# A fused linear-attention and MoE kernel on one core: another fixed order of its steps, and most weights' signs made by ScalarE

## The chip, the cores and the metric

The kernel runs on one core of a Trainium2 chip. Its time is the device time of one launch, in microseconds (us). Three runs of the kernel before took 515.26, 516.27 and 516.82 us; their median is 516.27 us.

## The reference, cut to what matters

For each of 4 x 8 heads a 48 x 48 state runs over 768 tokens; its output, put side by side over the heads, goes through one feed-forward layer.

```python
for t in range(S):                       # S = 768, per head, D = 48
    state = alpha[t][:, None] * state + outer(k[t], v[t])
    y[t] = q[t] @ state
x = y as (3072 tokens, 384)
h = x @ w_in                             # (384, 2048)
sp = maximum(h, 0) + log1p(exp(-abs(h)))
g = h * erf(sp)
out = g @ w_out                          # (2048, 384)
```

`w_in` and `w_out` are float64 and come to the chip as pairs of 32-bit words.

## The kernel before, in words

The program is one flat list of steps, written out in the string `ORDER`. A step is a method and its indices, and most are one instruction, or one block of matmuls. The loop at the end walks the list. `Queue` ties each instruction of TensorE (PE), VectorE (DVE), ScalarE (ACT) and SyncE (SP, which issues the loads and stores) to the one before it on its engine, so the list fixes the order on each engine. Between engines only data and buffers decide.

**Attention.** There are 24 chunks (64 tokens of two batches each); the step's index is the chunk. `la lk lq lv` load alpha, k, q, v. On DVE `sb` and `sa` are the scans of alpha, `kk` and `qq` scale k and q, `mk` masks the scores, `td` and `ta` decay the state and add to it. On PE `pn` transposes k, `ps` makes the scores (32 matmuls), `qt` and `sv` the two parts of the output (64 each), `pu` the state's update (32). `xh` (ACT) rounds the output to x_hi. The rest x_lo is either one subtraction on DVE (`xl`), or two matmuls with minus identity that take x_hi off in PSUM (`xp`, PE) and a copy (`xe`, ACT).

**Feed-forward.** Two chunks make a block of 256 tokens; there are 12 blocks, the first index of the MoE's steps; the second is one of 4 groups of 512 hidden columns, the third a half of a group. `hm` is 18 matmuls (three products of hi and lo parts), evicted from one of two PSUM buffers by `he` (ACT) or `hd` (DVE). Then, per group, ACT runs `u` (tanh), `n1 n2 n3` (ln, ln, exp) and `g` (gelu), and DVE `ma mb z1 z2`, all on 128 x 1024. `ga` (ACT) or `gd` (DVE) rounds a half, `gl` (DVE) makes the rest of it, and `om` is 12 matmuls into the output's accumulators: 4 with gh and wo_hi, 4 with gh and wo_lo, 4 with gl and wo_hi. `oe` (ACT) or `ob` (DVE) evicts an accumulator, `od` stores it. `u` and `g` need one table set of ACT, `n1 n2 n3` another; `need` puts a table load wherever the list goes over from one to the other.

**Weights.** `wl` loads a piece, 12 of `w_in` (i, 512 columns) and 16 of `w_out` (o, 384 columns). From the 64-bit words a piece is put together: `wy` (ACT) takes exponent and mantissa from the high word, `wc` (ACT) or `wv` (DVE) the three bits from the low word, `wa` (DVE) joins them by a shift and an or, `wb` (DVE) ors the sign in. Then `wh` (ACT) or `wk` (DVE) rounds to hi, and lo comes from `wq` (DVE), or from `wp` (three matmuls in an `hm` buffer, PE) and a copy `we` (ACT). Methods `wd` and `wf` are in the class, but no step of the list before calls them: `wd` (ACT) writes the high word, scaled, as float16 into the upper 16 bits of each word, which sets the sign there, and `wf` (ACT) writes the three bits as int16 into the lower 16 bits. With both, `wb` is not needed.

`dw_n` runs n matmuls that compute nothing used. `f1 f2 f3` make the flag that the end of the program branches on.

Of the kernel before, what the change touches and what calls it, by code (L numbers as in the profile page):

```python
# [41 lines left out]
wqo_0 he_0_2_0 whi_10 wyo_1 wao_1 sb_4 wqi_9 n1_0_0 xh_2 xl_2 pn_2 kn_2 n2_0_0 wqi_10 ic_3 hm_0_1_1 he_0_1_1
n3_0_0 hm_0_2_1 he_0_2_1 wbo_1 rc_4 who_1 pu_2 ps_3 wlo_3 wyo_3 lq_4 lk_4 wlo_7 mk_3 ta_2 qt_3 ma_0_0 g_0_0 sa_4
wlo_6 mb_0_0 wqo_1 hm_0_3_0 z1_0_0 wco_3 wao_3 lv_3 sv_3 xh_3 xl_3 kk_4 pn_3 he_0_3_0 wyo_7 hm_0_3_1 kn_3 ic_4
z2_0_0 td_4 lk_5 he_0_3_1 la_5 wco_7 wco_6 hm_1_0_0 qq_4 wlo_9 wyo_6 sb_5 u_0_1 wao_7 wbo_3 ga_0_0_0 gl_0_0_0
hm_1_1_0 he_1_0_0 ga_0_0_1 gl_0_0_1 wao_6 u_0_2 n1_0_1 pu_3 ps_4 n1_0_2 rc_5 n2_0_1 qt_4 om_0_0_0 hm_1_0_1 wbo_7
who_7 mk_4 ta_3 lv_4 sv_4 sa_5 td_5 who_3 wqo_3 kk_5 n3_0_1 he_1_1_0 ma_0_1 wbo_6 pn_4 wqo_7 mb_0_1 he_1_0_1
n2_0_2 kn_4 lq_5 qq_5 n3_0_2 who_6 ma_0_2 la_6 xh_4 xl_4 om_0_0_1 wyo_9 wco_9 wao_9 wqo_6 mb_0_2 g_0_1 z1_0_1
wlo_11 wyo_11 hm_1_2_0 he_1_2_0 wbo_9 lk_6 z2_0_1 lv_5 hm_1_3_0 he_1_3_0 g_0_2 z1_0_2 pu_4 wco_11 ps_5 mk_5 lq_6
wlo_8 wco_8 wyo_8 wlo_4 z2_0_2 qt_5 wao_8 ga_0_1_1 wlo_5 hm_1_3_1 he_1_3_1 hm_1_2_1 wco_4 wlo_13 wyo_4 wao_11  # L50
u_0_3 gl_0_1_1 hm_1_1_1 wlo_10 u_1_0 wbo_8 ta_4 ga_0_2_0 om_0_1_1 wbo_11 sv_5 ic_5 who_9 wqo_9 who_8 n1_0_3
gl_0_2_0 wqo_8 om_0_2_0 sb_6 he_1_1_1 lv_6 wao_4 td_6 ga_0_1_0 gl_0_1_0 pn_5 wbo_4 xh_5 he_1_2_1 rc_6 xl_5
hm_2_1_0 hm_2_1_1 wyo_5 who_11 wqo_11 wco_5 wko_4 sa_6 wao_5 qq_6 qt_6 kn_5 pu_5 wyo_10 wlo_14 wco_10 wbo_5
wao_10 kk_6 ps_6 n2_0_3 ga_0_2_1 n1_1_0 who_5 wqo_5 he_2_1_0 wqo_4 om_0_1_0 n3_0_3 gl_0_2_1 wbo_10 ma_0_3
he_2_1_1 wvo_13 hm_2_0_0 mb_0_3 n2_1_0 wyo_13 n3_1_0 wao_13 mk_6 ta_5 wbo_13 who_10 wqo_10 g_0_3 z1_0_3 he_2_0_0
hm_2_0_1 who_13 wqo_13 z2_0_3 wco_14 ma_1_0 pn_6 he_2_0_1 wyo_14 wlo_15 wco_15 wyo_15 wao_14 om_0_2_1 kn_6 sv_6
ga_0_3_0 gl_0_3_0 pu_6 wao_15 ga_0_3_1 gl_0_3_1 xh_6 wbo_14 lv_7 om_0_3_0 u_1_1 lk_7 wbo_15 g_1_0 mb_1_0
hm_2_2_0 ic_6 la_7 who_15 wqo_15 who_14 wqo_14 om_0_3_1 u_1_2 n1_1_2 oe_0_1 od_0_1 oe_0_0 hm_2_2_1 z1_1_0 z2_1_0
ga_1_0_0 sb_7 lq_7 rc_7 gl_1_0_0 gd_1_0_1 n1_1_1 lq_8 xl_6 sa_7 gl_1_0_1 om_1_0_0 n2_1_2 n2_1_1 om_1_0_1
he_2_2_0 qq_7 kk_7 hm_2_3_0 n3_1_1 td_7 ma_1_1 mb_1_1 n3_1_2 he_2_2_1 ps_7 mk_7 qt_7 hm_2_3_1 g_1_1 u_1_3 z1_1_1  # L60
z2_1_1 u_2_1 ic_7 ga_1_1_0 sv_7 xh_7 ta_6 la_8 ga_1_1_1 lv_8 ma_1_2 pn_7 gl_1_1_0 om_1_1_0 gl_1_1_1 om_1_1_1
sb_8 he_2_3_0 mb_1_2 g_1_2 n1_1_3 he_2_3_1 n2_1_3 n3_1_3 lk_8 xl_7 hm_3_0_0 hm_3_0_1 z1_1_2 z2_1_2 rc_8 gd_1_2_0
gl_1_2_0 om_1_2_0 ma_1_3 he_3_0_0 ga_1_2_1 gl_1_2_1 om_1_2_1 g_1_3 he_3_0_1 td_8 hm_3_1_0 hm_3_1_1 mb_1_3 sa_8
u_2_0 n1_2_0 lk_9 n2_2_0 z1_1_3 z2_1_3 gd_1_3_1 kk_8 ga_1_3_0 la_9 gl_1_3_0 om_1_3_0 n3_2_0 lq_9 qq_8 kn_7
n1_2_1 n2_2_1 n3_2_1 he_3_1_0 od_0_0 he_3_1_1 gl_1_3_1 pu_7 ps_8 ma_2_0 qt_8 mb_2_0 om_1_3_1 sb_9 ma_2_1 mb_2_1
g_2_1 z1_2_1 ob_1_0 od_1_0 u_2_2 oe_1_1 hm_3_2_0 mk_8 z2_2_1 hm_3_2_1 g_2_0 ic_8 rc_9 gd_2_1_1 u_2_3 n1_2_2 sv_8
gd_2_1_0 gl_2_1_1 gl_2_1_0 xh_8 n2_2_2 ta_7 om_2_1_0 pn_8 z1_2_0 he_3_2_0 ic_9 sa_9 om_2_1_1 he_3_2_1 z2_2_0
gd_2_0_1 gl_2_0_1 n3_2_2 n1_2_3 kk_9 xl_8 lv_9 ma_2_2 hm_3_3_0 hm_3_3_1 ga_2_0_0 n2_2_3 n3_2_3 kn_8 qq_9 g_2_2
om_2_0_1 mb_2_2 td_9 qt_9 pu_8 ps_9 ma_2_3 gl_2_0_0 om_2_0_0 u_3_1 u_3_0 z1_2_2 he_3_3_1 mk_9 sv_9 g_2_3
he_3_3_0 lq_10 n1_3_0 z2_2_2 gd_2_2_0 gl_2_2_0 om_2_2_0 od_1_1 la_10 mb_2_3 gd_2_2_1 xh_9 sb_10 xl_9 hm_4_0_0  # L70
rc_10 n1_3_1 n2_3_1 n2_3_0 gl_2_2_1 n3_3_0 n3_3_1 sa_10 he_4_0_0 ta_8 ma_3_0 hm_4_0_1 he_4_0_1 om_2_2_1 g_3_0
z1_2_3 z2_2_3 ga_2_3_0 mb_3_0 u_3_2 ga_2_3_1 z1_3_0 hm_4_2_0 hm_4_2_1 ma_3_1 lk_10 kk_10 u_3_3 qq_10 he_4_2_0
la_11 gl_2_3_0 g_3_1 n1_3_3 pn_9 kn_9 gl_2_3_1 n2_3_3 n3_3_3 om_2_3_0 td_10 om_2_3_1 oe_2_1 oe_2_0 qt_10 lk_11
z2_3_0 mb_3_1 z1_3_1 hd_4_2_1 z2_3_1 gd_3_1_0 sb_11 gl_3_1_0 ga_3_0_1 pu_9 ps_10 mk_10 ta_9 gl_3_0_1 n1_3_2
n2_3_2 n3_3_2 ic_10 rc_11 ic_11 hm_4_1_0 he_4_1_0 lv_11 hm_4_1_1 td_11 he_4_1_1 om_3_1_0 ma_3_2 pn_10 ga_3_0_0
gl_3_0_0 u_4_0 om_3_0_1 od_2_1 g_3_2 sa_11 u_4_1 mb_3_2 z1_3_2 ga_3_1_1 ma_3_3 g_3_3 lq_12 gl_3_1_1 z2_3_2
hm_4_3_0 hm_4_3_1 om_3_1_1 om_3_0_0 u_4_2 n1_4_2 ga_3_2_1 kd_10 lv_10 pu_10 n1_4_1 n2_4_1 kk_11 la_12 mb_3_3
lq_11 qq_11 ps_11 sv_10 xh_10 sb_12 he_4_3_1 gl_3_2_1 om_3_2_1 gd_3_2_0 gl_3_2_0 mk_11 ta_10 rc_12 xl_10 z1_3_3
z2_3_3 gd_3_3_1 od_2_0 pn_11 n1_4_0 n2_4_0 om_3_2_0 kn_11 gl_3_3_1 n3_4_0 ga_3_3_0 gl_3_3_0 qt_11 ma_4_0 pu_11
sa_12 n3_4_1 lk_12 mb_4_0 sv_11 he_4_3_0 n2_4_2 ma_4_1 xh_11 xl_11 lk_13 mb_4_1 kk_12 om_3_3_1 n3_4_2 g_4_1  # L80
td_12 g_4_0 la_13 z1_4_1 z1_4_0 z2_4_1 om_3_3_0 ob_3_0 od_3_0 u_4_3 qq_12 hm_5_0_0 he_5_0_0 hm_5_0_1 he_5_0_1
u_5_0 n1_5_0 z2_4_0 ga_4_0_0 gd_4_0_1 hm_5_1_0 lv_12 he_5_1_0 ma_4_2 mb_4_2 hm_5_1_1 oe_3_1 he_5_1_1 od_3_1
gl_4_0_0 qt_12 n1_4_3 ps_12 mk_12 hm_5_2_0 om_4_0_0 gl_4_0_1 sb_13 lq_13 hm_5_3_0 n2_4_3 ic_12 ta_11 n3_4_3
ma_4_3 pn_12 lk_14 he_5_2_0 n2_5_0 n3_5_0 mb_4_3 kk_13 ma_5_0 g_4_3 mb_5_0 ga_4_1_1 td_13 gl_4_1_1 u_5_1
om_4_0_1 he_5_3_0 hm_5_2_1 g_4_2 he_5_2_1 rc_13 sa_13 z1_4_2 hm_5_3_1 om_4_1_1 g_5_0 gd_4_1_0 gl_4_1_0 om_4_1_0
la_14 z1_4_3 z2_4_2 gd_4_2_0 kn_12 gl_4_2_0 u_5_2 n1_5_1 lq_14 ic_13 z2_4_3 sv_12 n2_5_1 ga_4_2_1 om_4_2_0 xh_12
xl_12 qq_13 gl_4_2_1 pu_12 ps_13 n1_5_2 n3_5_1 ma_5_1 qt_13 mk_13 g_5_1 mb_5_1 z1_5_1 ga_4_3_1 gl_4_3_1 om_4_2_1
lv_13 sv_13 xh_13 xl_13 he_5_3_1 z2_5_1 ga_4_3_0 gl_4_3_0 sb_14 om_4_3_1 ta_12 td_14 n2_5_2 lv_14 n3_5_2
hm_6_1_0 he_6_1_0 hm_6_2_0 he_6_2_0 rc_14 sa_14 ic_14 qq_14 ma_5_2 pn_13 kn_13 mb_5_2 u_5_3 z1_5_0 z2_5_0
ga_5_1_1 g_5_2 om_4_3_0 oe_4_0 oe_4_1 od_4_1 hm_6_0_0 he_6_0_0 hm_6_0_1 n1_5_3 n2_5_3 lk_15 hm_6_1_1 n3_5_3  # L90
kk_14 z1_5_2 z2_5_2 gl_5_1_1 pu_13 ps_14 la_15 hd_6_0_1 u_6_0 hd_6_1_1 hm_6_2_1 he_6_2_1 mk_14 ta_13 gd_5_2_0
# [855 lines left out]
```

## Time and profile before

| | us |
|---|---|
| median of three runs | 516.27 |
| span of the profiled execution, first to last instruction | 513.9 |
| median less span (what lies around it) | 2.4 |
| PE busy | 504.0 |
| weight loads of PE (PEld) busy | 481.7 |
| DVE busy | 488.2 |
| ACT busy | 465.8 |

The clock granted to TensorE was 1.00 of full speed in the whole span. Three engines are busy for over nine tenths of the time. A busy PE in this profile is one with a matmul under way, so what a step costs is read from the start of one to the start of the next, not from its length. An instruction of DVE or ACT is recorded until its last write, and the next one starts about 0.1 us before that.

### The profile page before, as it was taken

To read this page: it belongs to the slowest core of one execution; us is meant where nothing else is said; L and a number is where in the kernel's file an instruction comes from. 1 tells how busy PE (TensorE), PEld (TensorE's weight loads), DVE (VectorE), ACT (ScalarE), POOL (GpSimd) and SP (SyncE) were. 2 spreads that over 40 slices of the span, in tenths; PEclk is the share of its full clock that TensorE was granted. 3 is DMA by queue.
4 is the path that set the end of the run, shared out by engine and by line. 5 is a ranking of instruction groups with operands and counts; after the bars stand their busy time and mean duration, and the time that the engine had idled before them with its cause. 6 is when DMAs were issued, how large, how long until landed. Compare 5 with 4: busy or idle time off the path is not lost.

```text
span 513.9 us, 16869 instructions
## 1 busy us (share of the span) xinstructions
PE 504.0 (98%) x7465; PEld 481.7 (94%) x7465; DVE 488.2 (95%) x655; ACT 465.8 (91%) x637; POOL 6.5 (1%) x41
## 2 busy tenths in 40 slices
...
GB/s 324 401 200 176 117 188 131 97 81 60 58 74 44 22 99 78 45 73 83 23 78 107 80 41 60 85 15 44 68 111 54 90 58 32 3 1 32 0 32 34
DMA packets 21387, 43.69 MB, mean 85 GB/s; under 512 B 2368, under 2 KB 5440, under 8 KB 21312
## 3 DMA queue, kind: packets, MB, share of 16 engines
...
q8 instruction: 59, 0.97, 0.8%
q14 instruction: 16, 0.13, 0.1%
...
## 4 chain that ended last, share of the span: by engine, by line
PE 64%; DVE 18%; ACT 12%; issue 4%; DMA 1%; POOL 1%; DVEq 0%; POOLq 0%; ACTq 0%
PE acc L211 29%; PE h__112 L211 13%; PE h__111 L211 12%; PE both L211 4%; PE py L211 4%; DVE t L211 2%; DVE gl__104 L211 1%; ACT L211 1%; DVE gl__103 L211 1%; DVE w__98 L211 1%; DVE w__100 L211 1%; PE warm L211 1%; ACT w__97 L211 1%; DMA s__87<-in_moe_w_out_dram 1%; DVE w__97 L211 1%
## 5 line engine op out<-in xcount | busy, mean ns | idle before, releaser
L211 ACT ACT_TABLE_LOAD x64 | 82.1, 1283 | 1.9 <-PEq L901 0.9
L211 PE MATMUL acc<-wo_hi,gh__102 128*128 128x384 f32 x192 | 44.7, 346 | 0.1
L211 PE MATMUL acc<-wo_hi,gh__101 128*128 128x384 f32 x192 | 43.9, 348 | 0.1
L211 PE MATMUL acc<-wo_lo,gh__102 128*128 128x384 f32 x192 | 43.0, 337 | 0.2 <-DVE wo_lo L211 0.2
L211 PE MATMUL acc<-wo_hi,gl__104 128*128 128x384 f32 x192 | 43.1, 337 | 0.0
L211 PE MATMUL acc<-wo_lo,gh__101 128*128 128x384 f32 x192 | 41.6, 336 | 0.0
L211 PE MATMUL acc<-wo_hi,gl__103 128*128 128x384 f32 x192 | 41.6, 337 | 0.0
L211 PEld LDWEIGHTS acc<-wo_lo,gh__102 128*128 128x128 f32 x192 | 34.2, 188 | 0.5 <-DVE wo_lo L211 0.5
L211 PEld LDWEIGHTS acc<-wo_hi,gl__104 128*128 128x128 f32 x192 | 34.3, 188 | 0.0
L211 PEld LDWEIGHTS acc<-wo_hi,gl__103 128*128 128x128 f32 x192 | 34.0, 188 | 0.2 <-DVE gl__103 L211 0.2
L211 PEld LDWEIGHTS acc<-wo_lo,gh__101 128*128 128x128 f32 x192 | 34.1, 188 | 0.0
L211 PEld LDWEIGHTS acc<-wo_hi,gh__101 128*128 128x128 f32 x192 | 31.6, 188 | 1.9 <-DVE gh__101 L211 0.4
L211 PEld LDWEIGHTS acc<-wo_hi,gh__102 128*128 128x128 f32 x192 | 32.6, 188 | 0.8 <-DVE gh__102 L211 0.2
L211 DVE TENSOR_TENSOR_SCAN B<-raw_a,back 128x520 f32<-128x520 f32 x24 | 29.6, 1233 | 4.0 <-POOL T L266 3.9
L211 DVE TENSOR_TENSOR_SCAN A<-raw_a,start 128x520 f32<-128x520 f32 x24 | 29.6, 1233 | 0.2
L211 ACT ACTIVATE s__88<-s__88 128x1024 f32<-128x1024 f32 x22 | 23.2, 1056 | 1.0 <-DVE t L211 0.9
L211 ACT ACTIVATE s__86<-s__86 128x1024 f32<-128x1024 f32 x20 | 21.2, 1058 | 1.9 <-DVE t L211 1.8
L211 PE MATMUL h__112<-x_hi__107,wi_hi 128*128 128x256 f32 x144 | 21.7, 286 | 0.3 <-ACT wi_lo L211 0.3
L211 PE MATMUL h__111<-x_hi__107,wi_hi 128*128 128x256 f32 x144 | 21.4, 284 | 0.0
L211 PE MATMUL h__111<-x_hi__108,wi_hi 128*128 128x256 f32 x144 | 21.1, 282 | 0.0
L211 PE MATMUL h__112<-x_hi__108,wi_hi 128*128 128x256 f32 x144 | 21.1, 282 | 0.0
L211 PE MATMUL h__112<-x_lo__109,wi_hi 128*128 128x256 f32 x144 | 21.0, 281 | 0.0
...
## 6 DMA issues: line engine op xcount, KB each, us to landing
...
raw_v__114<-in_v_dram SPq DMA_DIRECT2D x12, 256.0 KB, 3.6
out_dram<-o__106 SPq DMA_DIRECT2D x12, 192.0 KB, 2.0
...
```

The lines of the kernel that those rows point to most:

```text
L211: ins = made(*args, **kw)
```

## The change

The list is replaced by another one. Both have the same loads, stores and matmul blocks of attention and MoE, and each `hm`, `om`, `u`, `n1` to `n3`, `g`, `ma`, `mb`, `z1`, `z2`, `gl` once. These counts differ:

| steps (engine) | before | after |
|---|---|---|
| wc / wv / wd / wf, pieces of w_in | 12 / 0 / 0 / 0 | 0 / 3 / 9 / 9 |
| the same, pieces of w_out | 13 / 3 / 0 / 0 | 2 / 4 / 10 / 10 |
| wb (DVE), w_in + w_out | 12 + 16 | 3 + 6 |
| wh (ACT) / wk (DVE), w_in | 12 / 0 | 5 / 7 |
| wh (ACT) / wk (DVE), w_out | 15 / 1 | 9 / 7 |
| wp (PE) with we (ACT) / wq (DVE), w_in | 9 / 3 | 7 / 5 |
| xl (DVE) / xp (PE) with xe (ACT) | 24 / 0 | 18 / 6 |
| ga (ACT) / gd (DVE) | 51 / 45 | 43 / 53 |
| he (ACT) / hd (DVE) | 80 / 16 | 73 / 23 |
| kn (ACT) / kd (DVE), that copy k's transposes | 20 / 4 | 18 / 6 |
| oe (ACT) / ob (DVE) | 18 / 6 | 19 / 5 |
| matmuls of dw | 25 | 24 |
| goings-over between the two table sets | 63 | 79 |

One line of `hm` changes: the buffer of a group is now taken when the first of its halves comes, whichever that is.

This is how many steps of each kind stand in the list ahead of `hm_1_0_0`, the first matmuls of the second block:

| engine | before | after |
|---|---|---|
| PE | 8 hm, 9 wp, 4 pn, 4 ps, 3 pu, 4 sv, 2 qt, 25 dw | 8 hm, 7 wp, 4 pn, 5 ps, 4 pu, 4 sv, 2 qt, 3 xp, 24 dw |
| DVE, weights | 17 wa, 16 wb, 2 wv, 7 wq | 17 wa, 6 wb, 6 wv, 8 wk, 8 wq |
| DVE, the rest | 5 sb, 5 rc, 5 sa, 5 kk, 4 qq, 4 mk, 4 xl, 3 td, 1 ta, 1 each of ma mb z1 z2 | the same with 5 qq, 1 xl, no z2 |
| ACT, weights | 18 wy, 17 wc, 16 wh, 9 we | 18 wy, 1 wc, 10 wd, 10 wf, 7 wh, 7 we |
| ACT, the rest | 8 he, 4 kn, 4 xh, 5 ic, 2 ta, 3 table loads, 1 each of u n1 n2 n3 g | the same with 4 ic, 3 xe |

And this many, on PE ahead of `om_1_1_0`, on DVE up to and with `gl_1_1_0`, its last input:

| engine | before | after |
|---|---|---|
| PE | 24 hm, 10 om, 9 wp, 8 pn, 8 ps, 7 pu, 8 sv, 6 qt, 25 dw | 26 hm, 10 om, 7 wp, 9 pn, 10 ps, 9 pu, 9 sv, 7 qt, 6 xp, 24 dw |
| DVE, weights | 28 wa, 28 wb, 3 wv, 1 wk, 19 wq | 28 wa, 9 wb, 7 wv, 14 wk, 21 wq |
| DVE, attention | 8 each of sb rc sa kk qq mk, 7 xl, 6 td, 5 ta | 10 each of sb rc sa kk qq, 9 mk, 2 xl, 7 td, 6 ta |
| DVE, MoE | 7 ma, 6 each of mb z1 z2, 1 gd, 11 gl | the same with 6 gd |

The diff, cut to the beginning and the end of both lists and the line of `hm`:

```diff
...
 ORDER = """
-la_0 wli_2 wyi_2 wci_2 wli_3 wyi_3 wci_3 sb_0 rc_0 sa_0 wai_2 wbi_2 whi_2 wli_0 wyi_0 wci_0 wai_3 wbi_3 dw_14
-wpi_2 lk_0 kk_0 wli_4 whi_3 wyi_4 lq_0 ic_0 la_1 wci_4 wei_2 wai_0 wbi_0 pn_0 kn_0 whi_0 wpi_3 wei_3 qq_0 dw_3
-ps_0 wai_4 wli_7 wci_7 wli_6 sb_1 mk_0 wyi_7 wbi_4 wai_7 wci_6 wyi_6 wli_8 wpi_0 rc_1 whi_4 dw_7 wpi_4 wbi_7
-whi_7 wai_6 sa_1 wbi_6 wyi_8 wci_8 wai_8 lv_0 ic_1 wei_4 wli_5 lq_1 qq_1 wei_0 lk_1 pu_0 kk_1 wli_1 lv_1 wci_5
-sv_0 xh_0 wyi_5 xl_0 wbi_8 wpi_7 wai_5 whi_6 ps_1 mk_1 wci_1 wyi_1 wai_1 whi_8 wei_7 wlo_2 wpi_6 wvo_2 sv_1
-wyo_2 xh_1 wbi_1 whi_1 wei_6 wpi_8 ta_0 la_2 sb_2 wao_2 wlo_12 wyo_12 dw_1 wpi_1 pn_1 wei_8 wbi_5 whi_5 wpi_5
-wli_11 wco_12 kn_1 wbo_2 wei_1 wli_9 who_2 rc_2 ic_2 xl_1 wei_5 sa_2 hm_0_0_0 wao_12 td_2 lq_2 wyi_11 wbo_12
...
-hd_11_3_0 hm_11_3_1 gl_11_0_1 om_11_0_1 od_10_1 g_11_1 z1_11_1 ga_11_0_0 gl_11_0_0 om_11_0_0 z2_11_1 gd_11_1_1
-he_11_3_1 u_11_3 n1_11_3 z1_11_2 gl_11_1_1 om_11_1_1 gd_11_1_0 z2_11_2 gl_11_1_0 f2 om_11_1_0 n2_11_3 n3_11_3
-ma_11_3 ga_11_2_1 f3 mb_11_3 gl_11_2_1 g_11_3 z1_11_3 od_10_0 om_11_2_1 ga_11_2_0 gl_11_2_0 om_11_2_0 z2_11_3
-gd_11_3_1 gl_11_3_1 om_11_3_1 ga_11_3_0 gl_11_3_0 om_11_3_0 oe_11_0 od_11_0 oe_11_1 od_11_1
+wli_2 la_0 sb_0 wli_0 rc_0 wfi_2 wyi_2 wli_3 wdi_2 wyi_0 wfi_0 wai_2 lk_0 sa_0 dw_3 dw_14 wki_2 wdi_0 wfi_3 kk_0 wai_0
+lq_0 qq_0 wyi_3 pn_0 wdi_3 kn_0 ic_0 wki_0 wli_6 wli_7 wai_3 wpi_2 wyi_6 ps_0 wli_4 wfi_6 wdi_6 wyi_7 wqi_0 wvi_7 la_1
+whi_3 mk_0 wai_6 dw_7 wai_7 lk_1 wei_2 wki_6 sb_1 lv_0 wpi_3 wfi_4 wbi_7 sv_0 wdi_4 wyi_4 wpi_6 rc_1 wli_10 lq_1 wki_7
+sa_1 kk_1 wei_3 qq_1 wai_4 wli_1 xh_0 pu_0 wvi_1 wpi_7 ps_1 wyi_10 wfi_10 lv_1 wei_6 ic_1 wli_8 la_2 wyi_1 wli_11
+wei_7 lk_2 wdi_10 wli_5 xp_0 wki_4 wai_1 lq_2 wli_9 wpi_4 xe_0 mk_1 sv_1 wfi_8 lv_2 wbi_1 ta_0 pn_1 wyi_8 sb_2 wai_10
+wlo_2 whi_1 rc_2 xh_1 td_2 wpi_1 sa_2 kn_1 xp_1 la_3 wei_4 wei_1 xe_1 wvi_5 wlo_0 wdi_8 pu_1 wyi_5 hm_0_0_0 hm_0_0_1
...
+ga_11_0_1 ma_11_2 mb_11_2 z1_11_1 oe_10_0 ob_10_1 gl_11_0_1 ga_11_0_0 hm_11_3_1 g_11_2 om_11_0_1 gl_11_0_0 om_11_0_0
+od_10_0 he_11_3_1 u_11_3 z1_11_2 z2_11_2 gd_11_2_0 n1_11_3 z2_11_1 gl_11_2_0 gd_11_1_1 n2_11_3 gl_11_1_1 om_11_2_0
+n3_11_3 od_10_1 om_11_1_1 ga_11_1_0 ma_11_3 gl_11_1_0 mb_11_3 f2 g_11_3 ga_11_2_1 z1_11_3 gl_11_2_1 z2_11_3 om_11_1_0
+gd_11_3_1 om_11_2_1 gd_11_3_0 gl_11_3_1 gl_11_3_0 om_11_3_1 om_11_3_0 oe_11_1 oe_11_0 od_11_1 f3 od_11_0
 """
...
@@ -531,7 +525,7 @@
 
         def hm(self, g, half):
             x_hi, x_lo = self.x
-            if half == 0:
+            if self.hs[g] is None:
                 self.hs[g] = self.pl.h.tile([P, GT * TB], F32, name="hs", tag="hs")
             self.ph = self.pl.ph.tile([P, 512], F32, name="ph", tag="h")
             n = 0
```

## Rows read from the trace of the kernel before

**Rows 1.** The page, part 1: busy time, share, instructions by engine.

```profile
PE 504.0 (98%) x7465; PEld 481.7 (94%) x7465; DVE 488.2 (95%) x655; ACT 465.8 (91%) x637; POOL 6.5 (1%) x41
```

**Rows 2.** Stretches: length, busy time (instructions) by engine, clock, DMA.

```profile
20.00:30.00 10.00, 9.35 (x126) 5.46 (x125) 10.00 (x19) 10.00 (x25) 0.00 (x0) 1.00 0.95 361
60.00:130.00 70.00, 69.73 (x1077) 67.02 (x1077) 69.11 (x103) 68.84 (x109) 0.30 (x3) 1.00 0.32 103
200.00:250.00 50.00, 50.00 (x862) 47.83 (x861) 49.07 (x63) 47.38 (x62) 0.30 (x3) 1.00 0.19 55
250.00:300.00 50.00, 49.98 (x822) 48.37 (x821) 48.28 (x65) 42.50 (x58) 0.20 (x2) 1.00 0.24 71
300.00:350.00 50.00, 49.87 (x697) 48.82 (x696) 48.49 (x62) 44.40 (x56) 0.20 (x2) 1.00 0.18 52
```

**Rows 3.** Timeline of 0 to 30: start, length, engine, instruction, [idle before].

```profile
3.92 1.24 DVE L211 TENSOR_TENSOR_SCAN B<-raw_a,back 128x520 f32<-128x520 f32 x1 [3.92 <-POOL T L266]
...
5.04 1.22 ACT L211 ACTIVATE w__97<-hs__90 128x512 f32<-128x512 f32 x2 [2.56 <-DMA hs__90<-in_moe_w_in_dram]
...
13.80 1.12 PE L211 MATMUL h__111<-w__99,ident 128*128 128x512 f32 x2
...
14.99 1.72 PE L211 MATMUL warm<-ident 128*128 128x128 f32 x14
...
28.88 0.99 PE L211 MATMUL h__112<-x_hi__107,wi_hi 128*128 128x256 f32 x6 [0.26 <-ACT wi_lo L211]
```

**Rows 4.** Timeline of 45 to 55.

```profile
52.90 0.87 PE L211 MATMUL h__112<-x_hi__108,wi_hi 128*128 128x256 f32 x6
```

**Rows 5.** Timeline of 118 to 128.

```profile
122.39 0.94 PE L211 MATMUL acc<-wo_hi,gh__101 128*128 128x384 f32 x4
...
122.82 0.68 DVE L211 TENSOR_TENSOR gl__103<-hs__93,gh__101 128x512 fp32r<-128x512 f32 x1
...
123.17 0.85 PE L211 MATMUL acc<-wo_lo,gh__101 128*128 128x384 f32 x4
...
123.56 1.06 ACT L211 ACTIVATE s__87<-s__87 128x1024 f32<-128x1024 f32 x1
...
123.86 0.86 PE L211 MATMUL acc<-wo_hi,gl__103 128*128 128x384 f32 x4
...
124.64 1.28 ACT L211 ACT_TABLE_LOAD   x1
...
125.93 1.06 ACT L211 ACTIVATE s__88<-s__88 128x1024 f32<-128x1024 f32 x1
...
126.64 0.87 PE L211 MATMUL h__112<-x_hi__108,wi_hi 128*128 128x256 f32 x6
...
127.34 0.87 PE L211 MATMUL h__112<-x_hi__108,wi_lo 128*128 128x256 f32 x6
```

**Rows 6.** Timeline of 160 to 200, PE alone.

```profile
184.57 0.86 PE L211 MATMUL py<-raw_q,T 48*32 48x64 f32 x64
185.35 0.57 PE L211 MATMUL both<-raw_v__114,kn 64*48 64x48 f32 x32
185.75 0.66 PE L211 MATMUL both<-raw_q,raw_k 48*64 48x64 f32 x32
186.34 0.97 PE L211 MATMUL h__112<-x_hi__107,wi_hi 128*128 128x256 f32 x6
```

**Rows 7.** Groups by line: count, busy us, mean ns, idle before.

```profile
L211 DVE SCALAR_TENSOR_TENSOR w__100<-w__100 128x384 int32<-128x384 int32 x10 | 5.5, 549 | 0.0
...
L211 DVE SCALAR_TENSOR_TENSOR w__98<-w__98 128x512 int32<-128x512 int32 x6 | 4.1, 676 | 0.0
...
L211 DVE CAST gh__101<-hs__94 128x512 fp32r<-128x512 f32 x5 | 2.1, 423 | 0.1
```

**Rows 8.** Timeline of 500 to 514.

```profile
509.88 0.49 ACT L211 ACTIVATE o__106<-acc 128x384 f32<-128x384 f32 x1 [0.55 <-PE acc L211]
510.40 0.33 SPq L211 DMA_DIRECT2D out_dram<-o__106  x1
```

More of the change, by code (lines that the diff above doesn't have):

```diff
@@ L42 @@
[L42 to L91, printed above, removed]
```

139 lines of the change are left out of this document (92 added, 47 removed).

## The prediction

> **What bounds the kernel now.** I read the busy shares first. PE, DVE and ACT are all over nine tenths busy [rows 1], so a share names no bound; the stretches show who is full when. Between 20 and 30 us DVE and ACT are busy for 10.00 of 10 while PE is not, and from 60 to 130 us DVE has 69.11 of 70 [rows 2]. From 200 to 350 us PE is full, DVE nearly, and ACT has slack: 2.6 + 7.5 + 5.6 = 15.7 us [rows 2].
>
> A full PE that runs late and a full PE that runs on time look alike, so I weigh its list. The prices of its steps are the distances from start to start: hm 2.13 (6 matmuls in 0.70 to 0.71), om 2.09 (4 in 0.69 to 0.70) [rows 5]; qt and sv 0.78, pu 0.40, ps 0.59 [rows 6]; wp 1.19 and a matmul of dw 1.72 / 7 = 0.25 [rows 3]; pn 0.35, an estimate from pu, which has eight times as many matmuls of less than half the columns. What the clock shows beyond the work listed so far is PE's lag. Ahead of hm_1_0_0 the counts give 8 hm 17.0, 9 wp 10.7, 25 dw 6.2, 4 pn 1.4, 4 ps 2.4, 3 pu 1.2, 4 sv 3.1, 2 qt 1.6, together 43.5; it starts at 52.9 [rows 4], lag 9.4. Ahead of om_1_1_0 the same sum is 110.1 and it starts at 122.4 [rows 5], lag 12.3. So PE lost 3 us in between. The second of these rows tells who kept it: the third product of that om starts at 123.86, and its input gl was finished by DVE at 122.82 + 0.68 = 123.50 [rows 5]. With DVE full, gl can't come earlier: up to there DVE's queue paces PE. That is the place to ask what the new list asks of DVE.
>
> **The change, part by part.** An instruction of DVE costs its mean less about 0.08: 0.60 with 512 columns, 0.47 with 384, and 0.34 for a copy of 512 from SBUF to SBUF [rows 7], by proportion 0.27 for 384; a scan 1.15 [rows 3]. A weight step of ACT is half of 1.22, less the overlap, 0.57 for 512 [rows 3] and an estimated 0.45 for 384 by proportion.
>
> *DVE up to hm_1_0_0.* Ten fewer wb (nine of 512) -5.9; four more wv +1.3; eight wk +2.7; wq five and three for three and four +0.7; three fewer xl -1.4; no z2 -1.1; one more qq +0.6: -3.1. Against it the scan sb_0 comes later: alpha's load stood first in the queue, and DVE began at 3.92; now a weight stands ahead of it, and the second load let its user begin at 5.04 [rows 3]: +1.1. So hm_1_0_0 can start near 52.9 - 3.1 + 1.1 = 50.9, if DVE decides. PE's own list ahead of it is 42.6 by the same prices (two wp, one dw fewer; one ps, one pu, three xp more), lag 8.3 for 9.4.
>
> *ACT up to there.* 16 fewer wc (12 of 512) -8.6; 10 wd and 10 wf (9 of 512 each) +11.2; nine fewer wh -4.9; two fewer we -1.1; three xe +1.3; one ic -0.1: about -2. It is not what decides, if wd and wf cost what wy and wc do. The trace has neither. From below I take what a copy of DVE costs, 0.34; from above an ACT instruction of twice the columns, 1.06 [rows 5]. I take 0.57, the nearest: the same input, the same count of elements, other bits out.
>
> *DVE up to gl_1_1_0.* 19 fewer wb (9 x 0.60 + 10 x 0.47) -10.1; five wv +1.3; 13 wk +4.0; two wq +1.2; five fewer xl -2.3; five gd +1.7; and, since the list brings attention forward, two each of sb, sa, rc, kk, qq, one mk, td, ta: +8.8. Together +4.6, while PE has 117.1 - 110.1 = 7.0 more of its own work ahead. gl then ends near 123.5 + 4.6 + 1.1 = 129.2, the om starts 1.47 ahead of its third product [rows 5], at 127.7, and PE's lag is 10.6 for 12.3. This is the gain: 1.7. It is larger than at hm_1_0_0 (1.1); I take 1.7, as the later place holds all that went before.
>
> *PE's own work, all of it.* Two wp fewer -2.4, one dw -0.25, six xp. An xp has two matmuls of 192 columns; nearest is one of 384 at 0.17 [rows 5], so between 0.1 and 0.5 with the hand-over; I take 0.25, +1.5. Sum -1.1.
>
> *The wait that xp adds.* xp waits for ACT's xh, and PE is in order: behind xp_2 stands hm_0_1_1, behind xp_5 hm_1_3_1, behind xp_6 hm_2_0_1. xh follows sv by a queue that was full (68.84 of 70 [rows 2]). Six such waits, each 0 to 0.5; I take 0.4 in all.
>
> *The table loads.* 16 more. Each holds ACT from 124.64 to 125.93, 1.29 us, and starts at the end of the one before, 123.56 + 1.06 [rows 5]: 20.6 us. The rest of ACT's account (wd, wf, xe against wc, wh, we, ga, he, kn) is some -6, so its busy time should rise by 14 to 15, to about 480. Counted by ACT's own work, 11 of the 16 fall between 200 and 320 us of it, 14.2 us, just where it has 15.7 to spare [rows 2]. I cost them at nothing; that slack hides them, and without it they are the third rival.
>
> The Trainium skill speaks against this part. "ScalarE: Activation LUTs", in "What ACT_TABLE_LOAD costs", prices a change of set as the load and a drain, some 2.66 us, and asks to batch by set. The load's length agrees with the trace; the drain does not show, since the load here follows directly. By the page the 16 would cost ACT 42.6 us.
>
> *The end.* Before, o of accumulator 0 was evicted while PE finished accumulator 1, whose eviction starts at 509.88, and the last store goes out at 510.40 [rows 8]. The last om still finishes accumulator 0 first, but now ACT has oe_11_1 ahead of oe_11_0: two evictions follow PE's end, +0.4 (0.49 less the overlap). If the flag's read on SP slips in between the two stores (f3 now stands there), up to 0.9. The chain from hm_11_3_1 to om_11_3 is unchanged, with six om beside it in both.
>
> *The line in hm* adds no instruction: nothing.
>
> *Sum.* -1.7 - 1.1 + 0.4 + 0.4 = -2.0. The span of 513.9 becomes 511.9; outside of it lie 2.4 us (the median of 516.27 less the span), which stay: **514.3 us**, 0.4% faster.
>
> **The rivals.**
>
> *The lag stays.* DVE's later start, or loads that come in another order, eat what the fewer wb give. For it: gl was ready 0.36 us before PE took it [rows 5], so DVE alone did not set the whole lag. Against: DVE's 69.11 of 70. Without the 1.7 the time is 516.0.
>
> *More is won.* After 122 us PE's lag grew further: at its last matmul's end, about 509.8 [rows 8], some 22. If the lower demand on DVE goes on until 200 us and half of what is lost there to waits is not lost, 2 to 3 us more: 511.8. Against it: PE is full from 200 us on.
>
> *ACT fills up (slower).* Between 200 and 350 us ACT's slack is not idle time at will: it is between instructions that wait for DVE and PE. If only half can be used, 14.2 - 7.9 = 6.3 us of the table loads are late; he then holds an hm buffer and PE stops. It decides once ACT's lag eats the 2 us or so by which he is ahead: +4.3, 518.6. For it: ACT at 480 of 512. Against: DVE asks less of PE in the same stretch.
>
> *wd and wf are dear.* At 1.06 each, 20 of them ahead of hm_1_0_0 add 9 us on an ACT with 2 to spare: +7, less what PE makes up, 520.
>
> *A drain with each change of set.* If the extra loads cost 2.66 in place of 1.29, that is 22 us more on an ACT with some 30 left over in the span, most of it in the wrong place: 522. The trace is against it.
>
> **How the numbers follow.** Forecast 0.44, its own range 512.6 to 515.8; the lag stays 0.20; more is won 0.12; ACT fills up 0.17; wd and wf dear 0.05; a drain 0.02. A measurement of this kernel tells 0.3% from no change, 1.5 us, so faster means under 514.7. From the forecast 0.31 lies there and 0.13 above; from "more is won" all 0.12; "the lag stays" is the same; the last three are slower. With a little of each across the borders: faster 0.43, same 0.33, slower 0.24. The range reaches into "more is won" and up to "ACT fills up", until two in ten are left out: 511.2 to 518.8.
>
> **What would show it.** Right: hm_1_0_0 near 51 and om_1_1_0 near 128; the first DVE scan near 5.0; wd and wf near 0.65 in length; 80 table loads of 1.28 and ACT near 480 busy; two evictions after PE's last matmul. Wrong: waits of PE for ACT (hs, x_hi) between 200 and 350 us; a lag at om_1_1_0 of 12 or more; 16-bit instructions of ACT near 1 us.

## The result and the profile after

The changed kernel takes **520.74 us** (520.53 to 521.15, 4 runs) against 516.00 (515.26 to 516.82, 4 runs) beside it: ratio 1.0094, 95% interval 1.0082 to 1.0106. It is 4.7 us slower where 2.0 us less was forecast. Its profiled execution took 520.65 us, with a span of 518.9 (513.9 before).

The page of the changed kernel, busy time by engine and one row of the queues (packets, MB, share of 16 engines):

```profile
PE 503.8 (97%) x7469; PEld 482.9 (93%) x7469; DVE 484.6 (93%) x665; ACT 479.8 (92%) x643; POOL 6.6 (1%) x41
...
q8 instruction: 59, 0.97, 0.8%
```

Beside [rows 1], DVE is 3.6 us less busy and ACT 14.0 more (14 to 15 were counted). PE is as busy as before, in a span 5 us longer: it stands still somewhere. The stretches that answer to [rows 2] (length, busy time and count by engine, clock, DMA):

```profile
20.00:30.00 10.00, 7.88 (x156) 5.34 (x154) 8.79 (x17) 8.31 (x19) 0.00 (x0) 1.00 0.95 338
60.00:130.00 70.00, 69.98 (x1316) 66.77 (x1314) 68.51 (x108) 69.28 (x112) 0.50 (x5) 1.00 0.36 115
200.00:250.00 50.00, 49.43 (x689) 48.17 (x688) 48.94 (x63) 49.63 (x62) 0.20 (x2) 1.00 0.16 46
250.00:300.00 50.00, 50.00 (x819) 48.50 (x818) 49.68 (x67) 48.85 (x59) 0.30 (x3) 1.00 0.25 76
300.00:350.00 50.00, 49.74 (x761) 48.48 (x762) 47.23 (x63) 47.48 (x59) 0.20 (x2) 1.00 0.22 68
```

Between 20 and 30 us DVE and ACT, both at 10.00 before, now have 1.2 and 1.7 us of idle time, and PE 2.1. When all three engines wait, none of them is the bound. PE's timeline there names what is:

```profile
20.69 0.68 PE L205 MATMUL both<-raw_q,raw_k 48*64 48x64 f32 x26
23.04 0.34 PE L205 MATMUL both<-raw_q,raw_k 48*64 48x64 f32 x6 [1.68 <-issue]
23.31 0.47 PE L205 MATMUL py<-x_hi__107,minus 128*128 128x192 f32 x2
23.62 1.04 PE L205 MATMUL h__111<-w__98,ident 128*128 128x512 f32 x2
24.10 0.80 PE L205 MATMUL h__111<-wi_hi,minus 128*128 128x512 f32 x1
24.82 0.86 PE L205 MATMUL py<-sT,raw_v__114 64*32 64x64 f32 x64
25.61 0.66 PE L205 MATMUL both<-ident,raw_k 128*128 128x128 f32 x4
26.10 1.02 PE L205 MATMUL h__112<-w__99,ident 128*128 128x512 f32 x2
26.56 0.80 PE L205 MATMUL h__112<-wi_hi,minus 128*128 128x512 f32 x1
27.20 0.36 PE L205 MATMUL py<-x_hi__107,minus 128*128 128x192 f32 x2
27.49 0.58 PE L205 MATMUL both<-raw_v__114,kn 64*48 64x48 f32 x32
28.00 0.97 PE L205 MATMUL h__111<-x_hi__107,wi_hi 128*128 128x256 f32 x6
28.81 0.75 PE L205 MATMUL h__111<-x_hi__107,wi_lo 128*128 128x256 f32 x5
30.38 0.38 PE L205 MATMUL h__111<-x_hi__107,wi_lo 128*128 128x256 f32 x1 [0.82 <-issue]
...
36.13 0.40 PE L205 MATMUL h__112<-x_hi__107,wi_hi 128*128 128x256 f32 x2
37.39 0.74 PE L205 MATMUL h__112<-x_hi__107,wi_hi 128*128 128x256 f32 x4 [0.86 <-issue]
```

Three times a step stops in the middle: ps_1 after 26 of its 32 matmuls, hm_0_0_0 after 11 of 18, hm_0_2_0 after 2. The operands of the matmul behind each stop were there: in the first two steps other matmuls had used them, and the piece of w_in that is new to the third matmul of hm_0_2_0 was rounded by ACT over 3 us before (by 33.2). So neither DVE nor ACT can be late, and the profile names nothing ("issue"). Count the matmuls between the first two stops: 6 + 2 + 2 + 1 + 64 + 4 + 2 + 1 + 2 + 32 + 6 + 5 = 127; the same count up to the third gives 126. With their weight loads that is some 254 instructions. The instruction queue moved 0.97 MB in 59 packets, 16.4 KB each; over PE's 2 x 7469 instructions it is 65 bytes an instruction, so a packet holds about 252 of them. PE stands at the end of a packet's worth of its own instructions. By the records of that queue a packet starts at 20.46, 28.03 and 35.03 us, and each time PE goes on 2.35 to 2.6 us later. The three stops hold 3.4 us of PE, and a fourth of 0.57 follows at 224.91. The kernel before has two small ones, 0.26 at 437.03 and this one in its own timeline:

```profile
21.59 0.35 PE L211 MATMUL both<-raw_q,raw_k 48*64 48x64 f32 x9 [0.19 <-issue]
```

The place of a stop goes by the count and not by the step. Counted from the first matmul in the trace, the three stops come behind matmuls 220, 347 and 473, and the 0.19 of the kernel before, whose list is another one, behind matmul 220 as well.

Where the time went, by the prediction's own reading (start time less PE's list by its prices): at hm_1_0_0, now at 55.90, the lag is 55.9 - 42.6 = 13.3 for 9.4; at om_1_1_0, at 133.54 below, 133.5 - 117.1 = 16.4 for 12.3. So 3.9 us are lost before 56 us, and between these two steps the lag grows by 3.1 as it did by 2.9. The last om starts at 511.43 for 507.60: with 1.1 less work another 0.8 of lag. Then the end, which answers to [rows 8].

The last om of the kernel before starts so:

```profile
507.60 0.51 PE L211 MATMUL acc<-wo_hi,gh__102 128*128 128x384 f32 x2
```

The changed kernel's timeline, DVE's first scan, hm_1_0_0, om_1_1_0 (answering [rows 5]), the last om and the end:

```profile
5.48 1.24 DVE L205 TENSOR_TENSOR_SCAN B<-raw_a,back 128x520 f32<-128x520 f32 x1 [5.48 <-DMA raw_a<-in_alpha_dram]
...
55.90 0.98 PE L205 MATMUL h__112<-x_hi__108,wi_hi 128*128 128x256 f32 x6
...
133.54 0.87 PE L205 MATMUL acc<-wo_hi,gh__101 128*128 128x384 f32 x4
...
134.00 0.69 DVE L205 TENSOR_TENSOR gl__103<-hs__93,gh__101 128x512 fp32r<-128x512 f32 x1
...
134.96 0.87 PE L205 MATMUL acc<-wo_hi,gl__103 128*128 128x384 f32 x4
...
511.43 0.52 PE L205 MATMUL acc<-wo_hi,gh__102 128*128 128x384 f32 x2
...
513.20 0.51 PE L205 MATMUL acc<-wo_hi,gl__104 128*128 128x384 f32 x2
513.75 0.49 ACT L205 ACTIVATE o__106<-acc 128x384 f32<-128x384 f32 x1 [7.77 <-PE acc L205]
514.14 0.48 ACT L205 ACTIVATE o__105<-acc 128x384 f32<-128x384 f32 x1
514.27 0.34 SPq L205 DMA_DIRECT2D out_dram<-o__106  x1
514.70 0.38 SPq L205 DMA_DIRECT2D out_dram<-o__105  x1
```

From PE's last matmul (513.71) to the end of the span are 5.2 us; before, from 509.84, 4.1. Sum: 3.9 + 0.2 + 0.8 - 1.1 + 1.1 = 4.9 of the 5.0 by which the span grew.

### The profile page after: what moved, and what is told of

It is laid out like the page before. It is cut to its first block, busy times and chain, and to the rows that moved or that the text cites. A ratio compares the mean times of both kernels' runs of the same rounds, so it can differ in the third digit from the quotient of the medians.

```text
span 518.9 us, 16931 instructions
## 1 busy us (share of the span) xinstructions
PE 503.8 (97%) x7469; PEld 482.9 (93%) x7469; DVE 484.6 (93%) x665; ACT 479.8 (92%) x643; POOL 6.6 (1%) x41
## 4 chain that ended last, share of the span: by engine, by line
PE 65%; ACT 21%; DVE 7%; issue 4%; DMA 2%; SPq 0%; DVEq 0%; ACTq 0%
PE acc L205 26%; PE h__111 L205 14%; PE h__112 L205 14%; PE py L205 5%; PE both L205 4%; ACT L205 4%; ACT s__86 L205 2%; ACT s__85 L205 2%; ACT w__97 L205 2%; ACT s__87 L205 2%; DVE t L205 2%; ACT s__88 L205 2%; DMA raw_v__113<-in_v_dram 1%; ACT w__98 L205 1%; ACT w__99 L205 1%
## 5 line engine op out<-in xcount | busy, mean ns | idle before, releaser
L205 PE MATMUL acc<-wo_hi,gh__101 128*128 128x384 f32 x192 | 43.2, 342 | 0.0
L205 PE MATMUL acc<-wo_hi,gh__102 128*128 128x384 f32 x192 | 43.0, 339 | 0.0
L205 PE MATMUL acc<-wo_hi,gl__104 128*128 128x384 f32 x192 | 42.7, 337 | 0.0
L205 PE MATMUL acc<-wo_hi,gl__103 128*128 128x384 f32 x192 | 42.1, 337 | 0.0
L205 PEld LDWEIGHTS acc<-wo_hi,gl__104 128*128 128x128 f32 x192 | 34.3, 188 | 0.0
L205 PEld LDWEIGHTS acc<-wo_hi,gl__103 128*128 128x128 f32 x192 | 34.2, 188 | 0.1
L205 PEld LDWEIGHTS acc<-wo_hi,gh__102 128*128 128x128 f32 x192 | 33.2, 188 | 0.1
L205 PEld LDWEIGHTS acc<-wo_hi,gh__101 128*128 128x128 f32 x192 | 32.4, 188 | 0.6 <-DVE gh__101 L205 0.3
L205 PE MATMUL h__111<-x_hi__107,wi_lo 128*128 128x256 f32 x150 | 22.1, 282 | 0.8 <-issue 0.8
L205 ACT ACTIVATE s__85<-s__85 128x1024 f32<-128x1024 f32 x20 | 21.1, 1057 | 1.8 <-DVE t L205 1.7
L205 PE MATMUL h__112<-x_hi__108,wi_hi 128*128 128x256 f32 x150 | 22.4, 285 | 0.3 <-DVE hs__90 L205 0.3
L205 ACT ACTIVATE s__87<-s__87 128x1024 f32<-128x1024 f32 x20 | 21.1, 1058 | 1.7 <-DVE t L205 1.4
L205 PE MATMUL h__112<-x_hi__108,wi_lo 128*128 128x256 f32 x150 | 22.1, 281 | 0.6 <-issue 0.6
L205 PE MATMUL h__111<-x_hi__107,wi_hi 128*128 128x256 f32 x150 | 22.4, 285 | 0.0
L205 PE MATMUL h__112<-x_hi__107,wi_hi 128*128 128x256 f32 x138 | 21.2, 288 | 0.9 <-issue 0.9
```

The costliest lines, as they stand in the source:

```text
L205: ins = made(*args, **kw)
```

## The experiments

All times stand against the kernel before, run beside them (medians 515.97 to 516.23). Three theories are tried: F, PE waits for its next 16 KB of instructions; L, the loads of the new list come late; W, wd and wf overfill ACT.

**Undoing parts of the list.** Fewer warm matmuls (which also moves the packets' ends by as many), alpha's load first, both, and the old signs in the new list:

```
fewer_dw     - dw_14            + dw_7
alpha_first  - wli_2 la_0       + la_0 wli_2
both         the two edits together
old_signs    - wf..  wd..       + wc.. , and wb behind wa
```

> The new list with dw_7 for dw_14: seven unused matmuls fewer, ahead of a stretch where PE waits for k anyway; every later instruction of PE stands 14 matmuls earlier in its stream. Theory F (PE stops at 23.0, 30.4 and 37.4 us because the next 16 KB of its instructions have not come; 1.8 + 1.0 + 1.1 us): the ends of the blocks fall elsewhere, the first into sv_1, the second and third behind hm work, so two of the three stalls go and the time falls by 2 to 3 us, to about 518. Theory L (the order of the loads made DVE and ACT late): 520.7, no change. Theory W (wd and wf overfill ACT): 520.7, no change.

> The new list with la_0 put ahead of wli_2, as in the old list; nothing else. Theory L: DVE's first scan starts near 3.9 in place of 5.5 and the time falls by about 1.5 us, to 519.2. Theory F: the three stalls of PE at its blocks' ends stay, PE gets its work no earlier, and the time stays within 0.5 us of 520.7. Theory W: no change.

> The new list with both edits: dw_7 for dw_14, and la_0 ahead of wli_2. If F and L are both true and add up: 520.7 - 2.5 - 1.5 = 516.7, about the time of the kernel before. If only F: 518. If only L: 519.2.

> The new list with the old way of making the weights' signs: each wf is a wc again, each wd is gone, and a wb stands behind the wa. ACT has 19 instructions (about 10 us) less, DVE 19 more (about 10 us). Theory W: ACT was overfull in the first 80 us, the time falls by 1 to 2 us, to 519 or less. Theories F and L: not faster; DVE has 10 us more in a stretch where it has little to spare, 520.7 to 523.

fewer_dw: 521.01 (518.27 to 522.79, 6 runs), 1.0079 [1.0049, 1.0110]. alpha_first: 520.54, 1.0100 [1.0071, 1.0129]. both: 518.41 (517.27 to 521.33), 1.0050 [1.0024, 1.0076]. old_signs: 527.18, 1.0217 [1.0200, 1.0234].

Neither edit pays by itself; together they give 2.3 us. In alpha_first the scan starts at 3.88 and PE is 1.1 us ahead at matmul 347, but the third stop grows from 0.86 to 1.35. In fewer_dw's trace the third stop still comes behind matmul 473, which is now 14 matmuls further on in the list (a listed one of dw is two in the trace), after the fourth of hm_0_2_0's last six. The first two stops are gone and another one stands behind matmul 600; together they hold 2.2 us in fewer_dw and 1.8 in both. That speaks for F, but fewer_dw's runs spread over 4 us, and its trace shows a second price. With seven warm matmuls fewer, PE waits 2.7 us for raw_k, and behind that wait the granted clock is at its lower level (0.5, or 1.2 GHz) for most of a stretch. fewer_dw, one window (columns as above):

```profile
10.00:14.00 4.00, 3.18 (x15) 1.73 (x19) 3.75 (x7) 3.91 (x9) 0.00 (x0) 0.57 1.02 404
```

So the times of these four runs did not separate F from L. old_signs speaks against W: the new signs save the new list 6.4 us.

**Cutting the suspected queue, and making the stop in the kernel before.**

```
short_after, short_before
+  for t in keep_s.tiles["s"]: nc.gpsimd.memset(t, 0.0)   # once, ahead of the steps
...
-  sp.dma_start(out=..., in_=...)
+  r = 32 if self.name in CUT else P
+  sp.dma_start(out=...[:r], in_=...[:r])
tiny_before  - wpi_5            + wpi_5 tiny_128
less_dve     - wbo.. (12, behind hm_1_0_0)
```

> The changed kernel, in which nine weight loads (wli_1, 8, 11, 5, 9 and wlo_2, 0, 6, 3) bring a quarter of their rows; the rest of these weights is left out of the computation, every instruction stays. By the trace of the changed kernel they are issued between 12 and 31 us and take some 10 us of a queue that is full until 36.7. Theory F (PE's next 16 KB of instructions wait behind queued loads): the packets that start at 28.03 and 35.03 start when PE reaches the 16 KB boundary, the stalls of 1.03 and 1.06 us ahead of hm_0_0_0 and in hm_0_2_0 go, that of 1.82 in ps_1 shrinks; 517 to 518.5. Theory L (the loads themselves come late): between 15 and 40 us only one wait on a load is left, 0.7 us, so 520 to 521, with the stalls where they were. If neither: about 520.7 with the stalls gone and their time idle for another engine's sake.

> The kernel before, in which the nine loads that take the same place in its queue (wli_5, 1, 11, 9, 10 and wlo_2, 12, 0, 1) bring a quarter of their rows; the rest of these weights is left out. Theory F: its only such stall is 0.2 to 0.3 us at 21.6, so 515.5 to 516.5. If shorter loads help for another reason (the port, the landing of the others), it gains as much as the changed kernel does, 2 us or more: 514 or less.

> The kernel before with 128 small matmuls (48 rows, 32 by 64) added after wpi_5, ahead of hm_0_0_0, where PE waits 0.4 us for ACT. By the rows of sv (64 in 0.8 us) they take 1.6 us. Theory F: the 16 KB boundary at matmul 347 falls among them near 28 us, and the next one 128 matmuls later near 29.5 in place of 37.4; the packet for it starts after 31 as before, so PE stands for 2 to 4 us more with nothing but instructions missing: 519 to 521. Without F: 0.8 to 1.6 us: 516.8 to 517.8 and no such stall.

> The kernel before without the wb steps of the output weights that are listed behind hm_1_0_0 (the sign of those weights' remainder is left out): 12 instructions of 0.47 us fewer for DVE, 5.6 us, most of them before 122 us. The prediction's theory (DVE's queue paces PE up to there): the lag at om_1_1_0 falls by up to 1.7 us and more, 514.5 or less. Theory H (PE's list is full, and the lag between 50 and 130 us is hand-overs of PE's own): 0 to 0.3, 515.9 to 516.3.

short_after: **518.12** (517.53 to 519.05, 7 runs), 1.0039 [1.0025, 1.0053]; short_before: 516.09, 0.9995 [0.9984, 1.0006]. A cut of nine loads gives 2.6 us where the stops are and nothing where they are not. PE's timeline in short_after has a remnant of the first stop and, at the places of the other two, none:

```profile
22.11 0.34 PE L205 MATMUL both<-raw_q,raw_k 48*64 48x64 f32 x6 [0.72 <-issue]
...
27.88 0.87 PE L205 MATMUL h__111<-x_hi__107,wi_lo 128*128 128x256 f32 x6
...
34.12 0.87 PE L205 MATMUL h__112<-x_hi__107,wi_hi 128*128 128x256 f32 x6
```

The packets start at 19.46, 25.56 and 29.46, for 20.46, 28.03 and 35.03. L is out for these loads: in the changed kernel no engine waits on any of them, and only one wait on another load shows between 15 and 40 us, 0.7 us for raw_v, which stays (0.66).

tiny_before: 521.18 (519.82 to 521.54), 1.0089 [1.0063, 1.0116]. The time lies where F put it, but not for the sum that I gave: a listed matmul of this kind is two in the trace, so the 128 are 256, and by the rows cost 4.0 us, not 1.6. The stop itself is there, in a kernel that has none at this place. Its timeline:

```profile
29.58 2.54 PE L206 MATMUL warm<-ident 48*32 48x64 f32 x164
33.05 1.53 PE L206 MATMUL warm<-ident 48*32 48x64 f32 x92 [0.93 <-issue]
34.51 0.99 PE L206 MATMUL h__112<-x_hi__107,wi_hi 128*128 128x256 f32 x6
```

It is 0.9 us, among matmuls whose only input is a constant, and ends 2.36 us after a packet that starts at 30.69. It is at the end of a packet's worth: matmul 347 of the trace is the 36th of the small ones, and the stop comes 128 matmuls behind it, after the 164th. What the loads do is put off the packet; how many instructions PE runs through in that time decides whether it matters.

less_dve: 515.91 (515.44 to 516.55, 10 runs), 0.9995 [0.9985, 1.0004]. DVE has 4.5 us less to do where [rows 2] showed 69.11:

```profile
60.00:130.00 70.00, 69.89 (x1075) 67.48 (x1076) 64.59 (x92) 69.04 (x108) 0.40 (x4) 1.00 0.32 105
```

and PE gains 0.3 us there: from hm_1_0_0 (53.80; this execution runs 0.9 late from 34 us on, ahead of all that is left out) to om_1_1_0 (122.97) are 69.2 us, for 69.5 before. gl still ends 0.37 us ahead of its matmul (124.10 and 124.47), so that row tells nothing of who paces whom. DVE's queue does not pace PE there. More work for DVE is another matter: in old_signs, with some 10 us more, PE waits for it (1.4 us for raw_q at 22.5).

**The loads put off in earnest, the signs alone, no table loads.**

```
late_loads   alpha_first, and wli_11 wli_9 wlo_2 behind la_3,
             wlo_0 wlo_6 wlo_3 behind la_4, their steps 8 to 28 places later
new_signs    (kernel before)  - wc..  wb..    + wf.. wd..
one_table    - AF.Ln, AF.Exp; need(LNEXP)     + AF.Tanh; need(GELU)
```

> The kernel alpha_first in which the loads wli_11, wli_9 and wlo_2 stand behind la_3 and wlo_0, wlo_6, wlo_3 behind la_4, with the steps of these weights 8 to 28 places later; nothing is left out. Theory F: the packet that follows the boundary at 22 us has 3 us less of loads ahead of it, so the stall in hm_0_0_0 (0.8 us in alpha_first) goes; ahead of the next one stand as many loads as before, so the stall in hm_0_2_0 (1.5 us) stays or halves; 518 to 519.7. If loads don't matter: 520.5 with both stalls. A rival of its own: ACT and DVE now wait for the late weights, 521 or more, with waits on loads of over 1 us between 30 and 50 us.

> The kernel before with the signs made the new way in its own order: wf and wd in place of each wc, no wb for those weights. Theory P (PE's list is full, ACT is the full one ahead of hm_0_0_0): nine weights ahead of it cost ACT 0.57 us more each, 5 us where ACT has 10.00 of 10, so PE waits for hi and lo of the last weights: 518 to 521. If the 16-bit signs pay by themselves, as DVE has 0.6 us less for each: 515 or less.

> The changed kernel with Tanh in place of Ln and Exp in n1, n2, n3, so that all functions come from one table set and some 80 table loads of 1.28 us go (the gelu's arithmetic is left out, the count of its instructions stays). The prediction's theory (the table loads lie in ACT's slack): 519.7 to 521. Rival (ACT fills up between 200 and 350 us and holds PE): 80 loads less, 514 to 517.

late_loads: 523.72 (522.06 to 527.42), 1.0160 [1.0112, 1.0209]. F's part came for the packet: the second one starts at 25.30, and the stop in hm_0_0_0 is gone. The time is the rival's, its sign is not: no engine waits on one of the late loads; the steps that I moved with them wait on one another. DVE's waits in late_loads (us in total, times, longest):

```profile
DVE w__97 L205 <- ACT w__97 L205: 6.2, 3, 3.0
```

The longest ends at 47.7 and lies where PE falls 2.8 us behind the changed kernel's trace (matmul 600 at 43.25 for 43.14, matmul 1000 at 65.67 for 62.86). And behind the first stop, which stays, the clock fell in the profiled execution, as its window shows:

```profile
23.00:26.50 3.50, 3.50 (x62) 1.89 (x57) 3.35 (x6) 2.58 (x5) 0.00 (x0) 0.52 0.65 236
```

That the stop in hm_0_2_0 is gone too may be the clock's doing: in end_swap (below), with the changed kernel's loads, the clock fell at the same place, and both later stops are missing.

new_signs: 529.48, 1.0259 [1.0242, 1.0276]. I had put the loss at 2 to 5 us; it is 13.5, as PE waits for a full ACT up to 115 us (1.3 us there, for kn), not only up to hm_0_0_0. Its first stretches, and then those of old_signs:

```profile
10.00:20.00 10.00, 7.73 (x67) 4.70 (x65) 5.62 (x10) 10.00 (x20) 0.00 (x0) 1.00 1.04 406
20.00:30.00 10.00, 6.88 (x202) 4.05 (x202) 7.06 (x11) 10.00 (x22) 0.00 (x0) 1.00 0.82 283
```

```profile
10.00:20.00 10.00, 8.49 (x160) 5.57 (x159) 9.90 (x18) 7.99 (x18) 0.00 (x0) 1.00 1.03 402
20.00:30.00 10.00, 7.80 (x154) 5.11 (x154) 9.93 (x17) 6.51 (x16) 0.00 (x0) 1.00 0.81 278
```

The new signs in the old list leave DVE idle behind a full ACT; the old signs in the new list leave ACT idle behind a full DVE. Each list is fitted to its signs, and neither half of the change can be judged alone.

one_table: 518.62 (518.30 to 519.78), 1.0058 [1.0041, 1.0075]: 2.1 us less than the changed kernel. That is neither the nothing of the prediction nor the 4 to 7 of the rival in that expectation.

**What was left open: the end, and whose the 2.1 us are.**

```
end_swap          - oe_11_1 oe_11_0 od_11_1 f3 od_11_0
                  + oe_11_0 oe_11_1 od_11_0 f3 od_11_1
both_end          both, with the same
one_table_before  (kernel before) as one_table
```

> The changed kernel with oe_11_0 ahead of oe_11_1 and the store of accumulator 0 first, as before. The prediction's theory (both evictions after PE's last matmul cost one eviction less its overlap): 0.4 less, 520.3. By the two traces (5.2 us from PE's end to the end of the span in place of 4.1): 1.1 less, 519.6.

> The kernel both (alpha first, seven matmuls of dw fewer) with that end as well: if the end is worth 1.1 wherever PE ends, 517.3, still slower than before (516.1); by the prediction's 0.4, 518.0.

> The kernel before with Tanh in place of Ln and Exp in n1, n2, n3, so that its 64 or so changes of table set go (the gelu's arithmetic is left out). If a table load costs PE the same wherever it stands (2.1 us for 80 of them in the changed kernel), 514.5. If only the 16 more of the changed kernel, brought together between 200 and 350 us, hold PE: 515.5 to 516.3.

end_swap: 519.83 (518.99 to 520.41), 1.0075 [1.0062, 1.0088], 0.9 less. Its timeline ends in one eviction behind PE, as before:

```profile
512.62 0.52 PE L205 MATMUL acc<-wo_hi,gl__104 128*128 128x384 f32 x2
512.63 0.34 SPq L205 DMA_DIRECT2D out_dram<-o__105  x1
513.18 0.49 ACT L205 ACTIVATE o__106<-acc 128x384 f32<-128x384 f32 x1 [0.57 <-PE acc L205]
513.70 0.33 SPq L205 DMA_DIRECT2D out_dram<-o__106  x1
```

Its span ends at 517.3, 4.2 us after PE, where the changed kernel has 5.2. So the trace prices the end at 1.0; the 0.9 between the two times, whose intervals overlap, would not tell it from 0.4. both_end takes 517.25 (516.11 to 519.65, 12 runs), 1.0023 [1.0009, 1.0036], the best form of the new list that I found, and still not better than the kernel before. It is 1.2 less than both, which fits, inside the spread of either. In its profiled execution (519.17) the clock fell too, behind a stop of 1.6 us:

```profile
42.00:46.00 4.00, 4.00 (x33) 3.93 (x23) 3.71 (x7) 1.83 (x3) 0.00 (x0) 0.57 0.62 197
```

PE is level with both's at matmul 600 (41.56 and 41.55) and 1.55 us behind it at matmul 1000 (62.83 and 61.28). So a stop can cost more than its length.

one_table_before: 514.92 (514.08 to 516.31, 10 runs), 0.9978 [0.9969, 0.9987]: 1.2 less than the kernel before. So 64 table loads cost that list 1.2 us and 80 cost the new one 2.1. The difference, 0.9, would be what the new list pays for more of them and for where they stand; by the intervals of the times it is uncertain by some 1.2 us either way. The traces bear out its sign: without the loads PE's matmul 7000 comes 2.1 us earlier in the changed kernel (446.71 for 448.81; level at matmul 2000, 114.28 and 114.26) and 0.6 in the kernel before (446.10 for 446.71; 121.09 for 121.41 at matmul 2000). One place of the cost, in alpha_first (waits between 200 and 340 us):

```profile
PE h__111 L205 <- ACT hs__94 L205: 0.4, 1, 0.4
```

It is at 225.83, where ACT evicts hs behind a table load. In the changed kernel's trace the stop of 0.57 at 224.91 stands just ahead of it in its place.

## Why the prediction was wrong

**The step that failed** is "up to there DVE's queue paces PE", and with it the gain of 1.7 in the lag. It rested on one row, gl ready 0.36 us ahead of its matmul, and on DVE's 69.11 of 70. A full engine beside a full PE shows only that the list keeps both fed: less_dve took 4.5 us from DVE, and PE gained 0.3. In the changed kernel gl ends at 134.69, 0.27 us ahead of its matmul, as close as before, though PE is late for another reason. What the lag grows by between the two steps, 2.9 and 3.1 us, is nearly the same in both lists; that it is PE's own hand-overs from step to step is argued, not shown. The lag at om_1_1_0 came out at 16.4, over the 12 that the prediction had named as a sign of being wrong.

**The term that was missing**: I asked of PE's list only what it costs, not how many instructions it has. In the new list attention comes forward, and its matmuls are small: qt has 64 in 0.78 us [rows 6], where 64 of an hm take 64 / 18 x 2.13 = 7.6. Two hundred and fifty instructions are then 6 to 7 us of PE in place of up to 10, while full DMA queues (0.95 in [rows 2] and above) hold the next packet back for some 5. In the kernel before, PE took 11.8 us, waits included, from matmul 220 (21.59) to matmul 347 (33.34); it ran through the next 126 in 3.8, but their packet had started at 31.67. short_after prices the missing term at 2.6 us; by the timeline the three stops hold 3.4.

**The end** was right in mechanism and too small: 0.4 forecast, 1.0 to 1.1 by the traces (0.9 by the times). The second eviction costs 0.4, the second store goes out 0.43 us behind the first, and the span ends 4.2 us after the last store's start where it was 3.5.

**The table loads at nothing** were too cheap, by about 0.9 as far as the times tell. The counts held (80 loads of 1.283 us, ACT 479.8 for "about 480"), and no drain shows: in [rows 5] the load starts 0.02 us behind the instruction before it, and the next one 0.01 behind the load. By what the Trainium skill states in "ScalarE: Activation LUTs", section "What ACT_TABLE_LOAD costs", load and drain together, the 16 more would by estimate have cost ACT 42.6 us; ACT's whole busy time rose by 14.0, and taking all 80 loads away was worth 2.1 us of the kernel's time. The rival *ACT fills up* had one right place (alpha_first shows it at 225.8 us) and, against 0.9, a price nearly five times too high.

**The start** was worse than forecast: DVE's first scan at 5.48 where 5.04 was expected (3.92 before), since the second load landed later than [rows 3] had it; raw_k then held DVE 1.2 us more.

**What held:** wd and wf cost about what wy and wc do; the changed kernel's groups on ACT (mean ns of one behind the busy time):

```profile
L205 ACT ACTIVATE w__99<-hs__92 128x512 int16<-128x512 uint8 x2 | 1.6, 810 | 0.0
L205 ACT ACTIVATE w__99<-hs__92 128x512 f16<-128x512 f32 x2 | 1.5, 774 | 0.0
...
L205 ACT ACT_TABLE_LOAD x80 | 102.6, 1283 | 2.2 <-PEq L895 0.9
```

They are 0.12 to 0.16 longer than the 0.65 expected (all groups of 512 columns lie between 0.75 and 0.84), far from the 1.06 of the rival. The xp waits are small, as assumed: the longest wait of PE for x_hi is 0.2 us. PE's own work, 1.1 less, is a count and was not measured by itself; an xp takes 0.3 in the timeline above (23.31 to 23.62) for the 0.25 assumed.

**What stays open.** Of the 4.7 us, 2.6 are missing instructions, 0.9 to 1.1 the end, some 0.9 the table loads (not clear of the noise), -1.1 PE's list (a count); some 1.3 are left. The traces put them ahead of hm_0_0_0: the late first loads and the remnant of the first stop (short_after still has a lag of 130.6 - 117.1 = 13.5 at om_1_1_0 for 12.3). No run measured them alone, as in alpha_first the stops ate what the early scan gave. What starts an instruction packet is not in the trace; that it stands in line behind queued loads is read from short_after and late_loads, where it started earlier with fewer loads ahead.
